# Sinkhorn-sorted attention feeding a top-1 expert layer: first sorting weights by 0/1 matmuls, later votes summed on GpSimd, TensorE order grouped by tile shape

## The chip, the cores and the metric

The kernel runs on one core of a Trainium2 chip. The metric is the device time of one execution in microseconds (us), given as the median of several runs. A core has five engines: TensorE (PE in the profile, with its weight loads as PEld), VectorE (DVE), ScalarE (ACT), GpSimd (POOL) and SyncE (SP). TensorE writes to PSUM, which has eight banks.

## The reference

```python
P = sort_net                                   # (4, 8, 8, 8): batch, head, block, block
for _ in range(5):                             # Sinkhorn
    P = P - np.max(P, axis=-1, keepdims=True)
    P = np.exp(P)
    P = P / (np.sum(P, axis=-1, keepdims=True) + 1e-09)
    P = P / (np.sum(P, axis=-2, keepdims=True) + 1e-09)
k_sorted = np.einsum('bhij,bhjcd->bhicd', P, k_b)   # 8 blocks of 96 rows, head_dim 64
v_sorted = np.einsum('bhij,bhjcd->bhicd', P, v_b)
scores = scale * np.matmul(q_b, k_sb.transpose(0, 1, 2, 4, 3))
...                                            # softmax in each block, times v_sb
x = attn_out.transpose(0, 2, 1, 3).reshape(3072, 512)
logits = x @ w_gate                            # 8 experts
expert_idx = np.argmax(logits, axis=1)
out[mask] = gate_w[mask, None] * (np.maximum(x[mask] @ w1[e], 0.0) @ w2[e])
```

Four batches, eight heads and 768 positions give 3,072 tokens of 512 features. Each expert has 1,024 hidden units.

## The kernel before

**The work.** Each of the four batches goes through attention and then through one expert. All inputs are read through GpSimd's DMA queue and turned to bf16 on the way. For a batch the kernel transposes q on TensorE (L593), sorts k (L614) and v (L641) by matmuls whose 0/1 structure holds the sorting weights, computes the scores of block i for all heads (`s`, L671), takes their exponential on ScalarE (L680), multiplies by the sorted v (`a`, L687), divides on VectorE (L697, L698), and transposes the result (`t`, L706) into `xT`. `route` (L731 to L755) computes the gate.

**The vote.** The kernel doesn't wait for the routing to load an expert. It sums v over all rows (`vote sum`, 24 matmuls, L538), projects the sum on the gate (`vote pick`, L547), reads the index of the maximum (L554, L555), and loads `w1` and `w2` of that expert (L338, L341), which it uses for the whole batch. Tokens that chose another expert are counted at the end; only if there are any does a loop over all experts run. For this input it doesn't run.

**The expert.** `h` is xT times w1 (four L764 matmuls for each of eight tiles and two halves), then a relu (L774 on ScalarE, L776 on VectorE), then `o`, hT times w2 (L769, in runs of four), weighed by the gate (L780, L782) and stored.

**First batch's sorting weights.** The Sinkhorn loop (L445 on ScalarE, L449 to L452 on VectorE) leaves `snb`, with batch and head on 32 partitions. `add_pk` and `add_pv` put it on 128 partitions: `rep` (L472, L498) copies the rows by a matmul with `expand_k` or `expand_v`, `sel` (L476, L502) multiplies by a mask `kj` or `vj`, `pt` (L479, L505) sums over j, and a last product with `ksel` or `vh` gives `pk` (L485) and `pv` (L509).

**v relay.** Before v can be sorted, VectorE copies it into another layout, `vr` (L578): four pieces for the first batch, two for the later ones.

**What sets the order.** Every step is a `Task` with a cost for each engine that can run it, the tasks it follows, a priority, and the PSUM banks it opens and closes. `Plan.schedule` plays a list schedule with these costs, and `emit` writes the instructions of each engine in that order; each engine then runs its own list strictly in order. The priorities put batch b at 100 b and the expert of batch b at 100 (b + 1), so that the expert of one batch and the attention of the next are interleaved. Tasks with a priority below -900 hold their place against others. `emit` puts matmuls on a tile of zeros (`idle`, L79) into gaps of TensorE's planned time. The loads of GpSimd's queue are one chain (L855 to L865): q0, v0, k0 in three parts, v1, then w1 and w2 of batch 0, q1, k1, then w1, w2, v, q, k of each following batch.

**Tile shapes on TensorE.** q, k and v groups write 64 columns of the array at a time (128*64 in the profile), the scores read 64 rows (64*128), and the rest uses 128 rows or columns.

Of the kernel before, what the change touches and what calls it, by code (L numbers as in the profile page):

```python
# [8 lines left out]
F32 = mybir.dt.float32  # L9
# [9 lines left out]
class Task:  # L19


    def __init__(self, name, cost, run, after, prio, opens, closes, lands):
        self.name, self.cost, self.run, self.prio = name, cost, run, prio
        self.after = [t for t in after if t is not None]
        self.opens, self.closes, self.lands = opens, closes, lands
        self.engine = self.start = self.end = self.behind = None
# [9 lines left out]
class Plan:  # L36
# [3 lines left out]
           ("dve", "pe"): 0.2, ("act", "dve"): 0.06, ("dve", "act"): 0.06,  # L40
           ("pe", "pe"): 0.0, ("act", "act"): 0.03, ("dve", "dve"): 0.04}
    LOOK = {"pe": 0.1, "act": 0.15, "dve": 0.15, "pool": 0.0, "sp": 0.0}
    FIRM = -900

    def __init__(self, dma_at=2.1):
        self.tasks, self.free = [], {}
        self.bank = [0.0] * 8
        self.dma_free = dma_at
        self.order = []

    def add(self, name, cost, run, after=(), prio=0, opens=None, closes=None, lands=None):
        t = Task(name, cost, run, after, prio, opens, closes, lands)
        self.tasks.append(t)
        return t
# [14 lines left out]
    def emit(self, nc, idle, psum, begin, warm, until):  # L69

        held, at = [0.0] * 8, begin
        for t in self.order:
            if t.engine == "pe":
                while t.start < until and t.start - at > 0.5:
# [3 lines left out]
                    us = 0.43 if at < warm else 0.217  # L78
                    nc.tensor.matmul(out=psum[:, free[-1], :], lhsT=idle[:, :128], rhs=idle,  # L79
# [27 lines left out]
    def schedule(self):  # L107
# [11 lines left out]
        while open_:  # L119
# [19 lines left out]
            for t in open_:  # L139
# [7 lines left out]
                for e, us in t.cost.items():  # L147
                    s = max(self.free.get(e, 0.0), bank_at)
# [9 lines left out]
                per.setdefault(e, []).append((s, t.prio, seq[t], t, end))  # L158
# [8 lines left out]
            t.engine, t.start, t.end = e, s, end  # L167
            self.free[e] = end
            if t.lands is not None:
# [4 lines left out]
                else:  # L174
                    t.end = end + 1.8
# [20 lines left out]
def kernel(  # L196
# [57 lines left out]
    v_in = [sb([P, HB, D], BF16, f"v_in{i}") for i in range(2)]  # L254
    qT = [sb([P, P, CS], BF16, f"qT{i}") for i in range(2)]
    ksT = [sb([P, X, 2, HP], BF16, f"ksT{i}") for i in range(2)]
    vr = [sb([P, D // 2, HP, 2], BF16, f"vr{i}") for i in range(2)]
# [20 lines left out]
    vh = sb([P, 2 * H], F32, "vh")  # L278
# [5 lines left out]
    expand_k = sb([BH, BH, NB * CQ], BF16, "expand_k")  # L284
    expand_v = sb([BH, BH, NB * 2], BF16, "expand_v")
# [84 lines left out]
    for i in range(2):  # L370
        e = "dve" if i == 0 else "pool"

        def zero_vr(e, i=i):
            engines[e].memset(vr[i][:, :, HB:, :], 0.0)

        def zero_ksT(e, i=i):
            engines[e].memset(ksT[i][:, :, :, HB:], 0.0)

        pads["vr", i] = add(f"zero vr{i}", {e: 0.5 if i == 0 else 1.0}, zero_vr, prio=-900 if i == 0 else 5)
        pads["ksT", i] = add(f"zero ksT{i}", {e: 0.5 if i == 0 else 1.0}, zero_ksT, prio=-899 if i == 0 else 5)  # L380
    mk_idle = add("idle", {"dve": 0.27}, lambda e: nc.vector.memset(idle, 0.0), prio=-950)  # L381
# [37 lines left out]
    def mask(name, ns, run, after, prio, e="dve"):  # L419
        return add(name, {e: ns}, run, after, prio=prio)  # L420

    m_vh = mask("vh", 0.27, lambda e: nc.vector.reduce_sum(
        vh.rearrange("p (f h) -> p f h", f=2),
        ident.rearrange("p (h j f) -> p f h j", h=H, j=NB), axis=AX.X), [mk_ident], -500)
    m_vm = mask("vmask", 0.17, lambda e: nc.vector.tensor_add(vmask, vh[:, :H], vh[:, H:]), [m_vh], -499)
    m_kc = mask("kc", 0.26, lambda e: nc.vector.reduce_sum(
        kc, ident.rearrange("p (x c) -> p x c", c=CQ), axis=AX.X), [mk_ident], -498)
    m_kj = mask("kj", 0.18, lambda e: nc.vector.reduce_sum(
        kj, kc.rearrange("p (h j) -> p j h", j=NB), axis=AX.X), [m_kc], -497)
    m_ks = mask("ksel", 0.26, lambda e: nc.vector.reduce_sum(  # L430
        ksel, ident.rearrange("p (h j c) -> p h c j", h=H2, j=NB), axis=AX.X), [mk_ident], -496)
    m_vj = mask("vj", 0.27, lambda e: nc.vector.reduce_sum(
        vj, ident.rearrange("p (h j f) -> p j h f", h=H, j=NB), axis=AX.XY), [mk_ident], -495)

    def run_expand(t, n, lo, hi):
        nc.gpsimd.tensor_copy(t[:, lo:hi], ident[:BH, lo:hi, None].to_broadcast([BH, hi - lo, n]))

    ek0 = add("expand k0", {"pool": 0.5}, lambda e: run_expand(expand_k, NB * CQ, 0, H), [mk_ident], prio=FIRST + 4)
    ev0 = add("expand v0", {"pool": 0.4}, lambda e: run_expand(expand_v, NB * 2, 0, H), [mk_ident], prio=FIRST + 4)
    ek1 = add("expand k", {"pool": 1.2}, lambda e: run_expand(expand_k, NB * CQ, H, BH), [mk_ident], prio=5)  # L440
    ev1 = add("expand v", {"pool": 0.8}, lambda e: run_expand(expand_v, NB * 2, H, BH), [mk_ident], prio=5)

    last = sn_at
    for it in range(5):
        last = add(f"exp {it}", {"act": 0.27}, lambda e: nc.scalar.activation(sn, sn, ACT.Exp), [last], prio=-990)  # L445

        def norm(view, dst, it, way):
            nonlocal last
            last = add(f"sum {way}{it}", {"dve": 0.22 if way == "r" else 0.26}, lambda e: nc.vector.reduce_sum(  # L449
                red[:, :, 0], view, axis=AX.X), [last], prio=-990)  # L450
            last = add(f"inv {way}{it}", {"dve": 0.19}, lambda e: nc.vector.reciprocal(red, red), [last], prio=-990)
            last = add(f"mul {way}{it}", {"dve": 0.25}, lambda e: nc.vector.tensor_mul(  # L452
# [9 lines left out]
    def add_pk(bs, prio, after, eng="dve"):  # L462
# [5 lines left out]
        def run_rep(e):  # L468
            t = bank(rep)[:, :n * NB * NB].rearrange("p (g i) -> p g i", g=n)
            for g in range(n):  # L470
                h0 = bs[0] * H + g * H2
# [17 lines left out]
    def add_pv(bs, prio, after, eng="dve"):  # L489
# [5 lines left out]
        def run_rep(e):  # L495
            t = bank(rep)[:, :n * NB * NB].rearrange("p (g i) -> p g i", g=n)
            for g, b in enumerate(bs):
                nc.tensor.matmul(out=t[:, g], lhsT=expand_v[:, b * H:(b + 1) * H].rearrange("p h x -> p (h x)"),  # L498
# [8 lines left out]
        for g, b in enumerate(bs):  # L507
            pv[b] = sb([P, 2 * H, NB], BF16, f"pv{b}")
            pv_at[b] = add(f"pv{b}", {eng: 0.27 if eng == "dve" else 0.5}, lambda e, b=b, g=g: engines[e].tensor_mul(  # L509
# [3 lines left out]
    add_pv([0], -980, [ev0], "pool")  # L513
    add_pk([0], -981, [ek0])

    def u32(ap):
        return ap.bitcast(U32)
# [9 lines left out]
    def add_attention(b):  # L529
# [5 lines left out]
        def run_vsum(e):  # L535
            t = bank(vb)[:, :H]
            for c in range(0, HB, 2):
                nc.tensor.matmul(out=t, lhsT=v_in[i2][:, c:c + 2, :].rearrange("p c d -> p (c d)"),  # L538
                                 rhs=vmask, start=(c == 0), stop=(c == HB - 2))

        vm = sb([P, H], BF16, f"vm{b}")
        t1 = add(f"vote sum{b}", {"pe": 0.65}, run_vsum, [v_at[b], m_vm], A - 20, opens=vb)
        t2 = add(f"vote vm{b}", {"act": 0.2, "dve": 0.2}, lambda e: copy(e, vm, bank(vb)[:, :H]), [t1], A - 20, closes=vb)

        def run_pick(e):
            for h in range(H):
                nc.tensor.matmul(out=bank(lb)[:, :E], lhsT=vm[:, h:h + 1].to_broadcast([P, P]),  # L547
                                 rhs=wv[:, h, :], start=(h == 0), stop=(h == H - 1))

        t3 = add(f"vote pick{b}", {"pe": 0.25}, run_pick, [t2, wv_a, wv_b], A - 20, opens=lb)  # L550
# [6 lines left out]
        t4 = add(f"vote read{b}", {"dve": 0.45}, run_read, [t3], A - 20, closes=lb)  # L557
# [6 lines left out]
        w1_at[b] = add(f"load w1.{b}", {"pool": 2.2}, run_w1, [t4, *relu_of.get(b - 2, [])], A - 20, lands=2.0)  # L564
# [7 lines left out]
        old = vsort_of.get(b - 2, [])  # L572
        cut = D // 4 if b else D // 8
        for d0 in range(0, D // 2, cut):
            def run_relay(e, d0=d0):
                dst = u32(vr[i2])[:, d0:d0 + cut, :HB, 0]
                src = u32(v_in[i2])[:, :, d0:d0 + cut]
                engines[e].tensor_copy(dst, src.rearrange("p c d -> p d c"))  # L578
            relays.append(add(f"relay{b}.{d0}", {"dve": 0.5 if b else 0.27}, run_relay,
                              [v_at[b], pads["vr", i2], *old], A - 10))  # L580
        v_done[b] = [t1, *relays]
# [369 lines left out]
```

## Time and profile before

| | us |
|---|---|
| median of 3 runs (167.73 to 168.97) | 168.0 |
| the profiled execution as a run | 170.06 |
| its span, first to last instruction | 168.4 |
| TensorE busy | 152.8 |
| ScalarE busy | 97.6 |
| VectorE busy | 84.4 |
| GpSimd busy | 28.6 |

In the profile, a line such as `L641` is a line of the kernel before. A group of instructions gives the busy time, the mean of one, and what ended the idle time before it. Matmuls are pipelined, so their durations overlap: what a group costs TensorE is read from the start of one group to the start of the next. The trace also holds the packets of each DMA queue, those of the instruction queues among them; adding up the bytes of the software queue gives the time at which each load ended.

### The profile page before, as it was taken

The page shows a single profiled execution, that of the slowest core. Times are in us where ns is not written, and L with a number is a line of the kernel's source. Part 1 is how long each engine was busy: PE and PEld are TensorE (multiplying, and loading weights), DVE is VectorE, ACT ScalarE, POOL GpSimd, SP SyncE. Part 2 cuts the span into 40 slices and gives each one's busy share as a digit, 9 for nine tenths or more (in the row PEclk, how much of TensorE's full clock was granted, in tenths as well). Part 3 has the DMA queues.
Part 4 walks back from the last instruction along what each step waited for, and adds up shares of the span by engine and source line. Part 5 has one row for each costly group of instructions (what it writes and reads, how often), then busy time and mean ns, then how long its engine had stood idle before and what let it go on. Part 6 is the DMA issues. An engine that isn't in the chain of part 4 may idle for free.

```text
span 168.4 us, 5239 instructions
## 1 busy us (share of the span) xinstructions
PE 152.8 (91%) x2246; PEld 95.1 (56%) x2261; DVE 84.4 (50%) x232; ACT 97.6 (58%) x147; POOL 28.6 (17%) x64
## 2 busy tenths in 40 slices
PE   6998559999999999999998999969999999999970
PEld 2366438768556656665555665745556655645540
DVE  5869685666524984443229664433227744420010
ACT  3174575557757745586757653747758736646440
POOL 6994700771000000800000001200000000000000
PEclk9999985599999999999999999999999999999999
DMA  3999999999999961699999603799131012005041
GB/s 30 209 202 221 159 209 197 203 210 208 207 219 239 257 133 66 127 221 203 221 207 250 154 5 123 111 230 208 25 125 62 4 62 101 30 0 187 0 152 47
DMA packets 13770, 24.51 MB, mean 146 GB/s; under 512 B 1328, under 2 KB 6448, under 8 KB 13744
## 3 DMA queue, kind: packets, MB, share of 16 engines
q0 software_dynamic: 9568, 17.83, 59.1%
q1 hardware_dynamic: 4032, 6.19, 10.5%
q8 instruction: 19, 0.31, 0.7%
q10 hardware_dynamic: 144, 0.13, 0.2%
q14 instruction: 7, 0.06, 0.1%
HBM read 35.68 MB, written 6.29 MB: 249 GB/s over the span
## 4 chain that ended last, share of the span: by engine, by line
PE 70%; DMA 17%; issue 5%; POOL 2%; DVE 2%; ACT 1%; DVEq 0%; ACTq 0%; POOLq 0%
PE psum L764 23%; PE psum L769 22%; DMA v_in<-in_v_dram 11%; DMA k_in<-in_k_dram 7%; PE psum L687 5%; PE psum L706 4%; PE psum L671 4%; PE psum L641 4%; PE psum L614 2%; PE psum L593 2%; ACT ex L680 1%; PE psum L538 1%; PE psum L731 1%; POOL k_in L313 1%; DVE vs L300 1%
## 5 line engine op out<-in xcount | busy, mean ns | idle before, releaser
L764 PE MATMUL psum<-xT,w 128*128 128x384 bf16 x256 | 50.9, 331 | 0.0
L769 PE MATMUL psum<-w,hT 128*128 128x512 bf16 (+1 forms) x186 | 43.9, 370 | 1.2 <-issue 0.6
L780 ACT ACTIVATE o<-psum,gws 128x512 f32<-128x512 f32 (+1 forms) x24 | 16.3, 679 | 28.0 <-PE psum L769 26.4
L764 PEld LDWEIGHTS <-w 128*128 128x128 bf16 x256 | 21.7, 99 | 12.6 <-issue 0.5
L769 PEld LDWEIGHTS <-hT 128*128 128x128 bf16 x200 | 17.9, 98 | 17.5
L680 ACT ACTIVATE ex<-psum 128x768 bf16<-128x768 f32 x32 | 25.4, 810 | 3.4 <-PE psum L671 2.6
L774 ACT ACTIVATE hT<-psum 128x384 bf16<-128x384 f32 x42 | 20.6, 490 | 10.1 <-PE psum L764 10.0
L698 DVE TENSOR_TENSOR xo<-psum,rec 96x512 bf16<-96x512 f32 x32 | 22.0, 687 | 1.3 <-DVE rec L697 0.3
L776 DVE TENSOR_SCALAR hT<-psum 128x384 bf16<-128x384 f32 x22 | 12.3, 557 | 12.1 <-PE psum L764 11.9
L298 ACT CAST vs<-psum 128x1024 bf16<-128x1024 f32 x13 | 13.1, 1019 | 6.9 <-PE psum L641 6.1
L300 DVE COPY xT<-psum 128x384 bf16<-128x384 bf16 x28 | 9.9, 353 | 12.2 <-PE psum L706 11.4
L338 POOL DMA_DIRECT2D w<-in_moe_w_dram x4 | 3.2, 804 | 73.6 <-DVE xT L300 61.9
L687 PE MATMUL psum<-vs,ex 128*128 128x65 bf16 x256 | 14.1, 201 | 0.9 <-ACT ex L680 0.9
L687 PEld LDWEIGHTS <-ex 128*128 128x128 bf16 x256 | 12.1, 103 | 4.6 <-ACT ex L680 1.3
L697 DVE RECIPROCAL rec<-psum 96x8 f32<-96x8 f32 x32 | 6.4, 200 | 14.8 <-PE psum L687 14.6
L641 PE MATMUL psum<-pv,vr 128*64 128x64 bf16 x512 | 10.9, 198 | 3.1 <-issue 3.1
L298 ACT COPY qT<-psum 128x1024 bf16<-128x1024 bf16 x11 | 11.0, 1013 | 4.0 <-PE psum L593 2.1
L641 PEld LDWEIGHTS <-vr 128*64 128x64 bf16 x512 | 9.4, 112 | 6.3 <-issue 5.8
L706 PE MATMUL psum<-ident,xo 96*128 96x96 bf16 x128 | 11.6, 217 | 0.8 <-DVE xo L698 0.8
L706 PEld LDWEIGHTS <-xo 96*128 96x128 bf16 x128 | 8.3, 102 | 5.4 <-DVE xo L698 1.8
L671 PE MATMUL psum<-qT,ksT 64*128 64x96 bf16 x256 | 10.7, 213 | 0.4 <-DVE vs L300 0.4
L79 PE MATMUL psum<-idle 128*128 128x512 bf16 x29 | 9.6, 498 | 1.5 <-DVE idle L381 1.3
(90 smaller groups left out, 132.4 us busy)
## 6 DMA issues: line engine op xcount, KB each, us to landing
w<-in_moe_w_dram POOLq DMA_DIRECT2D x8, 1024.0 KB, 14.4
out_dram<-o SPq DMA_DIRECT2D x23, 256.0 KB, 2.9
q_in<-in_q_dram POOLq DMA_DIRECT2D x4, 768.0 KB, 20.3
v_in<-in_v_dram POOLq DMA_DIRECT2D x4, 768.0 KB, 15.5
k_in<-in_k_dram POOLq DMA_DIRECT2D x3, 768.0 KB, 26.6
k_in<-in_k_dram POOLq DMA_DIRECT2D x3, 256.0 KB, 10.3
out_dram<-o ACTq DMA_DIRECT2D x1, 128.0 KB, 3.2
out_dram<-o SPq DMA_DIRECT2D x1, 128.0 KB, 2.6
```

Of the source, the lines that this page charges most:

```text
L298: nc.scalar.copy(dst, src)
L641: nc.tensor.matmul(out=t[f * HP:(f + 1) * HP, u, :], lhsT=vr[i2][:, d // 2, :, d % 2], rhs=pv[b][:, f * H:(f + 1) * H, :].rearrange("p h i ...
L671: nc.tensor.matmul(out=sc[:, r, h4 * BLK:(h4 + 1) * BLK], lhsT=ksT[i2][rows, x].rearrange("p f c -> p (f c)"), rhs=qT[i2][rows, x * CQ:(x ...
L680: te = add(f"exp{b}.{i}", {"act": 0.82}, lambda e, ex=ex, sbk=sbk: nc.scalar.activation(ex[:, :H * BLK].rearrange("p (t c) -> p t c", t=2) ...
L687: nc.tensor.matmul(out=av[:, h // 4, h % 4, :], lhsT=ex[:, h * BLK:h * BLK + P], rhs=vs[i2][:, h * NB + i, :D + 1], start=(h % 4 == 0), st ...
L698: nc.vector.tensor_mul(xo, av[:, :, :, :D], rec.to_broadcast([BLK, 2, 4, D]))
L706: nc.tensor.transpose(out=tp[:, dc, :], in_=xf[:, dc * P:(dc + 1) * P], identity=ident[:BLK, :BLK])
L764: nc.tensor.matmul(out=ps, lhsT=w1t[:, dc, fc * P:(fc + 1) * P], rhs=xT[:, dc, half * NH:(half + 1) * NH], start=(dc == 0), stop=(dc == DC ...
L769: nc.tensor.matmul(out=ps, lhsT=hT[:, fc, s * P:(s + 1) * P], rhs=w2t[:, fc, d0:d1], start=(fc == 0), stop=(fc == FC - 1))
L774: nc.scalar.activation(dst, src, ACT.Relu)
L776: nc.vector.tensor_scalar_max(dst, src, 0.0)
L780: nc.scalar.activation(dst, src, ACT.Copy, scale=gw)
```

## The change

1. **First batch's weights.** `add_pv([0])` and `add_pk([0])` go. Three scratch tiles (in hT buffers that are still free) are set to zero on ScalarE (`zero first`, three copies), filled with ones in a shifted pattern on GpSimd (`fill k`, `fill v`), and eight matmuls for each tile, one for each j and summed in PSUM, give what `pt` held. VectorE multiplies straight from PSUM into `pk` and `pv`. `expand_k` and `expand_v` lose the first batch's part.
2. **Votes.** Batch 0 keeps its 24 matmuls, now with a fixed priority. For batches 1 to 3 GpSimd adds the 48 rows of v in six additions (`vote add`), and one matmul with 64 columns sums over partitions.
3. **Modes.** Each TensorE task has a mode (`full`, `col`, `row`). The schedule adds 0.09 to a task that changes it, and gives 12 of priority to one that stays in `col` or `row`.
4. **Relays.** For the first batch two of the four pieces go to GpSimd; the later ones stay on VectorE.
5. **Loads.** v1 is no longer fifth: it follows w1 and w2 of batch 0.
6. **Fillers and costs.** `emit` fills gaps from 0.25 on (before 0.5), with 128 columns where the gap is at most 0.5, up to 32 of planned time (before 26). Many costs and some priorities are set anew, and the zeroing of the first ksT goes to GpSimd.

```diff
+                while t.start < until and t.start - at > 0.25:
+                    n = 512 if t.start - at > 0.5 else 128
...
+                    if e == "pe" and t.mode != self.mode:
+                        us += self.SWITCH
...
+                stay = e == "pe" and t.mode == self.mode != "full"
+                per.setdefault(e, []).append((s, t.prio - self.STAY * stay, seq[t], t, end))
...
-    add_pv([0], -980, [ev0], "pool")
-    add_pk([0], -981, [ek0])
...
+    def zero_first(e, t, w):
+        nc.scalar.copy(t.rearrange("p (a w) -> p a w", a=NB), idle[:BH, None, :w].to_broadcast([BH, NB, w]))
...
+        def run_pt(e, t, rep):
+            for j in range(NB):
+                nc.tensor.matmul(out=bank(rep)[:, :NB], lhsT=t[:, j * P:(j + 1) * P], rhs=snb[:, :, j],
+                                 start=(j == 0), stop=(j == NB - 1))
...
+            pk_at[0, g] = add(f"pk0.{g}", {"dve": 0.29}, lambda e, t=t, g=g: engines[e].tensor_mul(
+                t, ksel[:, :, None, :].to_broadcast([P, H2, NB, CQ]),
+                bank(banks[g])[:, None, :NB, None].to_broadcast([P, H2, NB, CQ])), [at[g], m_ks], -982 + g, closes=banks[g])
...
+            def run_add(e):
+                tt = nc.gpsimd.tensor_add
+                n = HB // 2
+                tt(v_tmp, v_in[i2][:, :n], v_in[i2][:, n:])
+                while n > 3:
+                    n //= 2
+                    tt(v_tmp[:, :n], v_tmp[:, :n], v_tmp[:, n:2 * n])
+                tt(v_tmp[:, 0], v_tmp[:, 0], v_tmp[:, 1])
+                tt(v_sum[i2], v_tmp[:, 0], v_tmp[:, 2])
...
+            def run_vsum(e):
+                nc.tensor.matmul(out=bank(vb)[:D, :H], lhsT=v_sum[i2], rhs=vmask, start=True, stop=True)
...
+            cost = {"dve": 0.82} if b else {"pool": 0.76} if d0 >= D // 4 else {"dve": 0.48}
...
-    seq.remove(v_at[1])
-    chain.append(v_at[1])
-    chain = chain[:5] + [v_at[1]] + seq
+    chain += seq
...
-    plan.emit(nc, idle, psum, 1.3, 5.5, 26.0)
+    plan.emit(nc, idle, psum, 1.4, 5.6, 32.0)
```

In the order that results, TensorE's list of the main part has q groups of 48 matmuls and v groups of up to 128 in a row where before they stood between L764 groups, and the scores come in groups of up to 24.

## The prediction

> **What bounds the kernel.** I read the page's header and slices first, then busy time by stage, then the timeline of TensorE, then the DMA packets added up by load.
>
> ```profile
> span 168.4 us, 5239 instructions
> ...
> PE 152.8 (91%) x2246; PEld 95.1 (56%) x2261; DVE 84.4 (50%) x232; ACT 97.6 (58%) x147; POOL 28.6 (17%) x64
> ...
> PE   6998559999999999999998999969999999999970
> ...
> PEclk9999985599999999999999999999999999999999
> ```
> TensorE is nearly full everywhere except around slices 4 to 6, and its clock is halved around slices 6 to 8.
>
> ```profile
> 20.30:24.26 3.96, 2.63 (x63) 1.87 (x60) 3.55 (x7) 3.90 (x6) 0.00 (x0) 1.00 1.11 209
> 24.26:34.50 10.24, 8.97 (x139) 7.25 (x140) 6.97 (x21) 4.27 (x7) 3.82 (x6) 0.50 1.16 200
> 34.50:41.00 6.50, 6.50 (x193) 5.06 (x191) 3.78 (x9) 4.58 (x8) 3.31 (x9) 1.00 1.09 209
> 41.00:163.20 122.20, 118.23 (x1571) 71.31 (x1581) 54.49 (x142) 76.10 (x114) 5.74 (x9) 1.00 0.62 135
> ```
> Columns: stretch, length, busy PE, PEld, DVE, ACT, POOL, clock, DMA share, GB/s. From 41 us to the last matmul at 163.2 TensorE alone sets the time: 118.2 of 122.2. The 10.24 us from 24.26 run at clock 0.50. The last output store after 163.2 costs 5.2.
>
> ```profile
> 99.84 0.76 PE L538 MATMUL psum<-vmask,v_in 128*128 128x8 bf16 x24
> 100.46 0.33 PE L706 MATMUL psum<-ident,xo 96*128 96x96 bf16 x4
> ...
> 105.32 0.81 PE L764 MATMUL psum<-xT,w 128*128 128x384 bf16 x4
> 106.06 0.70 PE L641 MATMUL psum<-pv,vr 128*64 128x64 bf16 x32
> 106.69 0.34 PE L706 MATMUL psum<-ident,xo 96*128 96x96 bf16 x4
> 106.87 0.81 PE L764 MATMUL psum<-xT,w 128*128 128x384 bf16 x4
> ...
> 111.00 0.61 PE L641 MATMUL psum<-pv,vr 128*64 128x64 bf16 x25
> 113.08 0.31 PE L641 MATMUL psum<-pv,vr 128*64 128x64 bf16 x7 [1.47 <-issue]
> ```
> From start to start: a vote sum takes 0.62; four L764 matmuls take 0.65 before a group of the same shape and 0.74 before the 64-column groups. Over all groups after 41 us, leaving a shape for another costs 0.09 to 0.10 and entering 0.01 to 0.02, so about 0.105 a change. The 1.47 is a hole inside one group of 32, with no wait in it.
>
> **What the skill says.** "TensorEngine Tiling (Array Packing)", Key Properties: changing the tiling mode drains TensorE. The trace agrees (0.105). "Runtime: NRT & Kernel Launch", Instruction fetch mechanics: instructions come in blocks of 256, by DMA, while the present block runs. The trace agrees and adds a price: the holes at 17.4, 24.2, 77.3 and 111.6 us all lie at instruction rows 448, 704, 2496, 3520 of TensorE's order, all 192 past a multiple of 256. The trace's records of the instruction queue show 16 KB fetches of 0.9 us, begun about 4 us after the previous boundary while data DMA runs (16.75, 23.06, 110.87) and at once where DMA is idle (after 120 us); TensorE goes on some 1.4 us after one lands. So a block under load can't follow its predecessor in less than about 6.4 us. "SBUF — State Buffer", Who interferes with whom: VectorE with two SBUF inputs and GpSimd reading SBUF exclude each other. The last L452 took 0.50 against a mean of 0.25 under a GpSimd copy, so the trace agrees.
>
> **The change, part by part.**
>
> *Mode grouping.* I classed each group in TensorE's order by its tile shape: 103 changes before, 73 after. 30 x 0.105 = 3.1 us. Nearly all lie in the full stage. Taken: -3.1.
>
> *Votes of batches 1 to 3.* 24 matmuls become one: 3 x (0.62 - 0.03) = -1.8. GpSimd gets 3,008 elements a vote in six adds. The trace has two-input GpSimd work only at 128 elements, 404 ns (L509). Bounds: 1.23 ns an element (slope of its copies, 300 ns at 128, 1086 at 768) gives 4.5 us; 3.16 (all 404 ns counted as elements) gives 9.5. "GPSIMD Engine Reference", 3.1 Elementwise, has about 2.6 cycles; at 1.2 GHz an estimate of 6.5 and six fixed parts of 0.14 (small memsets: 0.12) make 7.4. I take 7.4. It is in GpSimd's queue ahead of w1, w2 and the next v, q, k loads.
>
> *First batch's weights.* rep, sel and pt (0.2 + 0.29 + 0.29, then two of 0.25) become 24 matmuls (eight of L547 took 0.27 of issue: estimate 0.7) and products straight from PSUM. The chain gains some 0.5. But the first zero copy, about 1.05 us by a 1024-element ScalarE copy (1.01), sits between the table load's end (2.15) and the first exp, which started at 2.55: +0.65. Exp 4 no longer stands behind a qT copy: -0.9. Also the vote sum, formerly hidden at 11.95 us, now follows these matmuls: +0.6. And two relay pieces read SBUF on GpSimd from about 11.7, against the last sn products. Net: k sorting starts at about 14.1, as before. What follows waits for k's last third, landed 15.6 (L614 waited for it till 15.83), and for the fetch at row 448. That can't start later than the DMA's going idle at 15.6, so TensorE goes on at 15.6 + 0.9 + 1.4 = 17.9 (before 19.05). Four vs copies in a row on ScalarE (1.02 each) then put the first exp at about 21.3, as before (21.29). Taken: 0.
>
> *v1's load, no longer fifth.* It was issued at 8.00 and kept DMA full while the vote ran. Now w1 follows k, with nothing behind: the vote is read at about 15.5 (vm is behind three qT copies), plus 1.5 to issue as before (15.04 to 16.56), plus 1.9 to first bytes: DMA idle 15.6 to 18.9. By bytes of the queue w1 landed at 25.0, w2 30.4, q1 34.4, k1 38.2; now 24.2, 29.7, v1 33.8, q1 38, k1 42. TensorE used q1 at 40.4, k1 at 44.4; its new order puts them at about 44 to 47. Hidden. VectorE loses v1's relays (1.6) and a vote read from the first attention.
>
> *Half clock.* The fillers (10 of 128 columns, 0.5 us in all) are few beside the stage's dependency gaps, and 20.3:24.26 stays as thin as before. I leave the halved stage in. Removed there: the second vote sum and pick, at half speed 0.8 + 0.3; 0.4 above the count made already. Taken: -0.4.
>
> *Denser blocks.* With v and q grouped, the block of rows 2240 to 2496 holds 3.6 us of work, that of 3264 to 3520 4.3 us. Against 6.4 that is up to 2.8 + 2.1, where before 0.38 + 1.47 were lost: +3.0 at most, 0 if DMA is quiet. Half: +1.5.
>
> *Later w1 of batch 1.* Vote 1 is picked at about 47, w1 issued at 49 (before 30.4). With the old transfer times (k2's end 24.6 after w1's first bytes at 38.0) v2 lands at 66, q2 71, k2 76; TensorE wants k2 at about 76. It falls together with the fetch hole above. Taken: 0; 2 if both are late.
>
> Sum against the profiled span: 168.4 - 3.1 - 1.8 - 0.4 + 1.5 = 164.6. That execution took 170.06 as a run; the median of the runs shown is 168.0, 0.4 below its span. So 164.3 for the median (0.3 of rounding and tail left open).
>
> **The rivals.**
>
> *The clock holds* (0.25). For: VectorE in the halved stage waited 1.38 + 0.33 + 1.28 for TensorE, and 1.84 just after it, so the first attention could end up to 4.8 earlier at full speed, with w1 there at 24. Against: the fillers are few. 3.7 off: 160.6.
>
> *The saved work comes back as holes* (0.22). Both dense blocks stall in full (+1.5 above the sum) and k2 or VectorE, kept out by GpSimd's reads, costs 2 more: 167.8, within 1%. Against: at row 3520 DMA should be quieter, since k3 lands about 107.
>
> *GpSimd too slow, slower than before* (0.12). Place: the single matmul of the vote sum, which waits in TensorE's order with all behind it. Slack worked from the order: batch 1, adds begin about 38 (after nine products of 0.4) and TensorE arrives at 47.5: 9.5; batch 2, v2 at 66 to TensorE at 77: 11; batch 3 about 10. Each us beyond is lost three times. The gain of 3.8 is gone at (30.5 + 3.8)/3 = 11.4 us a vote; at 12.4 it gives 171. For: port exclusion both ways. Against: most VectorE inputs there are in PSUM.
>
> *The change doesn't do what it says* is not one: the orders show 73 changes and one matmul a vote.
>
> **How the numbers follow.** Likeliest: 164.3 (0.41), own range 162.5 to 166.3. About 1% is what a measurement here can tell from no change: 166.3 to 169.7. Faster: 0.41 x 0.92 + 0.25 + a little of the third case = 0.66. Same: 0.03 + 0.18 = 0.21. Slower: 0.13. The range reaches down to the clock case, 160.3, and up past the eaten gain, 168.8.
>
> **What would show it.** Right: single-matmul vote sums; L764 to L641 handovers fewer; TensorE's sum down by about 4; the halved stage still near 10 us; w1's first issue near 17 and the second near 49; holes of 1 to 3 us at rows 2496 and 3520. Wrong: no halved clock after 24 us (then about 160.6); a wait of TensorE for GpSimd's v_sum; adds above 11 us; a first exp of scores later than 22.3; a DMA wait before k2's matmuls longer than 2.

## The result and the profile after

The kernel after takes 173.87 us (median of 4 runs, 173.31 to 175.53) against 168.49 for the kernel before on the same chip: ratio 1.0324, 95% interval 1.022 to 1.0428. It was forecast at 164.3 and is slower. Ratios leave disturbed executions out, so they are not exactly the quotient of the medians beside them. The profiled execution took 173.76, with a span of 172.1.

The page of the kernel after, its header, slices and two of its groups:

```profile
span 172.1 us, 5205 instructions
...
PE   6879779993799999959999999489999999999970
...
PEclk9998799999579999996999999957999999999996
...
L594 POOL TENSOR_TENSOR v_tmp<-v_in 128x1536 bf16<-128x1536 bf16 x3 | 11.1, 3703 | 32.9 <-DMA v_in<-in_v_dram 32.9
...
L646 DVE COPY vr<-v_in 128x768 uint32<-128x768 uint32 (+1 forms) x8 | 14.5, 1849 | 3.8 <-DMA v_in<-in_v_dram 3.8
```

The same copies in the kernel before, the later batches' form alone:

```profile
L578 DVE COPY vr<-v_in 128x768 uint32<-128x768 uint32 x6 | 4.9, 826 | 3.2 <-DMA v_in<-in_v_dram 3.2
```

Counting slices from 0, the thin stage around slices 4 to 8 got better: no slice there is as thin as the 5 of before, and the stretch of 10.24 us at half clock is gone (one of 3.41 us now begins at 15.53, slices 3 and 4). In its place are three thin places (slices 9 and 10, 17, 25 and 26), one for each later batch, each with a lowered clock there or in the slice behind. And the relay copies (L646, one form of it the later batches') have become long: 1849 ns in the mean.

Busy time by stage, same stretches as before (length, PE, PEld, DVE, ACT, POOL, clock, DMA share, GB/s):

```profile
24.26:34.50 10.24, 9.99 (x155) 7.12 (x152) 8.05 (x21) 7.84 (x15) 3.31 (x9) 1.00 1.14 200
34.50:41.00 6.50, 5.54 (x133) 3.38 (x131) 5.38 (x5) 2.13 (x4) 4.85 (x2) 1.00 1.07 211
41.00:169.13 128.13, 117.64 (x1585) 73.93 (x1578) 64.39 (x136) 74.83 (x122) 28.38 (x32) 0.93 0.64 139
```

24.26 to 34.50 ran at full clock (0.50 before). From 41 us to the halved tail TensorE was busy 117.6 of 128.1, at a mean clock of 0.93, where before it was busy 118.2 of 122.2 at 1.00 (to its last matmul). So the time was gained in the first attention and lost, with interest, in three later places. The timeline shows two of these:

```profile
36.03 4.47 DVE L646 COPY vr<-v_in 128x768 uint32<-128x768 uint32 x2 [0.38 <-DMA v_in<-in_v_dram]
36.07 3.76 POOL L594 TENSOR_TENSOR v_tmp<-v_in 128x1536 bf16<-128x1536 bf16 x1 [2.09 <-DMA v_in<-in_v_dram]
37.42 1.21 PE L711 MATMUL psum<-pv,vr 128*64 128x64 bf16 x64
...
40.42 1.65 DVE L817 SCALAR_TENSOR_TENSOR key<-sh,rev 128x48 f32<-128x48 f32 x1
40.56 0.70 PE L711 MATMUL psum<-pv,vr 128*64 128x64 bf16 x32 [0.96 <-DVE vr L646]
...
44.20 1.06 PE L711 MATMUL psum<-pv,vr 128*64 128x64 bf16 x32 [2.94 <-DVE vs L310]
...
72.42 4.47 DVE L646 COPY vr<-v_in 128x768 uint32<-128x768 uint32 x2 [0.16 <-DMA v_in<-in_v_dram]
72.54 3.68 POOL L594 TENSOR_TENSOR v_tmp<-v_in 128x1536 bf16<-128x1536 bf16 x1 [14.85 <-DMA v_in<-in_v_dram]
...
76.95 1.92 PE L711 MATMUL psum<-pv,vr 128*64 128x64 bf16 x64 [2.13 <-DVE vr L646]
```

The landing of v releases two instructions at once: VectorE's relay and GpSimd's first addition. The first relay runs (0.84 us), the second lasts 3.7, until 0.7 after the end of the addition (in batch 3 it starts later and lasts 2.9). TensorE waits for its output, and later for a `vs` copy that stands behind it on VectorE. The next VectorE instruction with two SBUF inputs, L817, takes 1.65 (0.20 without additions beside it). By the clock records, stretches of 6.83, 3.41 and 6.83 us at half clock begin at 42.84, 76.97 and 111.10.

Two explanations fitted this best: the additions shut the relays out of a port (L, the lock), or the vote, now later, makes w1 and with it the next v land late, so that the holes are waits for a load (D, lateness). A third (M) was that the new order of TensorE's matmuls costs the time. v2 had landed at 52.5 before and landed at 71.4 after.

### The profile page after: what moved, and what is told of

The parts are those of the page before. It is cut to its first block, busy times and chain, and to the rows that moved or that the text cites. A ratio compares the mean times of both kernels' runs of the same rounds, so it can differ in the third digit from the quotient of the medians.

```text
span 172.1 us, 5205 instructions
## 1 busy us (share of the span) xinstructions
PE 152.1 (88%) x2222; PEld 97.4 (57%) x2222; DVE 92.9 (54%) x212; ACT 101.2 (59%) x164; POOL 54.7 (32%) x85
## 4 chain that ended last, share of the span: by engine, by line
PE 42%; DMA 30%; DVE 16%; issue 4%; ACT 2%; POOL 2%; POOLq 1%; DVEq 0%
DMA v_in<-in_v_dram 30%; PE psum L840 15%; PE psum L835 14%; DVE vr L646 8%; PE psum L661 3%; PE psum L711 3%; PE psum L683 2%; POOL w L351 1%; DVE red L456 1%; DVE sn L459 1%; PE psum L758 1%; DVE red L458 1%; PE psum L742 1%; POOLq L629 1%; DVE key L817 1%
## 5 line engine op out<-in xcount | busy, mean ns | idle before, releaser
L840 PE MATMUL psum<-w,hT 128*128 128x512 bf16 (+1 forms) x200 | 46.4, 376 | 0.0
L845 ACT ACTIVATE hT<-psum 128x384 bf16<-128x384 f32 x55 | 27.0, 491 | 17.5 <-PE psum L835 13.0
L851 ACT ACTIVATE o<-psum,gws 128x512 f32<-128x512 f32 (+1 forms) x21 | 14.2, 677 | 22.8 <-PE psum L840 18.0
L594 POOL TENSOR_TENSOR v_tmp<-v_in 128x1536 bf16<-128x1536 bf16 x3 | 11.1, 3703 | 32.9 <-DMA v_in<-in_v_dram 32.9
L711 PEld LDWEIGHTS <-vr 128*64 128x64 bf16 x512 | 11.7, 129 | 12.0 <-DVE vr L646 7.3
L646 DVE COPY vr<-v_in 128x768 uint32<-128x768 uint32 (+1 forms) x8 | 14.5, 1849 | 3.8 <-DMA v_in<-in_v_dram 3.8
L853 DVE TENSOR_SCALAR o<-psum,gws 128x512 f32<-128x512 f32 (+1 forms) x4 | 2.7, 683 | 24.8 <-PE psum L840 20.3
L310 DVE COPY xT<-psum 128x384 bf16<-128x384 bf16 x21 | 7.4, 353 | 10.1 <-PE psum L777 9.8
L597 POOL TENSOR_TENSOR v_tmp<-v_tmp 128x768 bf16<-128x768 bf16 (+2 forms) x9 | 10.7, 1185 | 0.7
L82 PE MATMUL psum<-idle 128*128 128x512 bf16 (+1 forms) x39 | 9.1, 383 | 1.9 <-DVE idle L389 1.3
```

Source lines behind the costliest of these rows:

```text
L594: tt(v_tmp, v_in[i2][:, :n], v_in[i2][:, n:])
L711: nc.tensor.matmul(out=t[f * HP:(f + 1) * HP, u, :], lhsT=vr[i2][:, d // 2, :, d % 2], rhs=pv[b][:, f * H:(f + 1) * H, :].rearrange("p h i ...
L840: nc.tensor.matmul(out=ps, lhsT=hT[:, fc, s * P:(s + 1) * P], rhs=w2t[:, fc, d0:d1], start=(fc == 0), stop=(fc == FC - 1))
L845: nc.scalar.activation(dst, src, ACT.Relu)
L851: nc.scalar.activation(dst, src, ACT.Copy, scale=gw)
```

## The experiments

The ratio is that to the kernel before on the same chip; a number of the first column stands for an experiment below.

| | votes 1 to 3 | order | v1's load | us | ratio, 95% interval |
|---|---|---|---|---|---|
| after | GpSimd | grouped | late | 173.87 | 1.0324 (1.022 to 1.0428) |
| 1 | TensorE | grouped | late | 164.2 | 0.9638 (0.9537 to 0.9738) |
| 1 again | TensorE | grouped | late | 164.75 | 0.9764 (0.9619 to 0.9909) |
| 2 | GpSimd, order of plan | grouped | late | 175.56 | 1.0361 (1.0274 to 1.0448) |
| 3 | TensorE, dead additions | grouped | late | 165.23 | 0.9734 (0.9667 to 0.9802) |
| 4 | GpSimd, relay on ScalarE | grouped | late | 165.07 | 0.9741 (0.9646 to 0.9837) |
| 5 | GpSimd after the relays | grouped | late | 167.23 | 0.9858 (0.9763 to 0.9953) |
| 6 | GpSimd | grouped | fifth | 171.16 | 1.0157 (1.0064 to 1.0251) |
| 7 | TensorE | ungrouped | late | 163.52 | 0.9715 (0.9642 to 0.9788) |
| 7 again | TensorE | ungrouped | late | 163.35 | 0.9744 (0.9648 to 0.9839) |
| 8 | before, votes on GpSimd | ungrouped | fifth | 173.24 | none |
| 9 | TensorE | grouped | fifth | 168.76 | 1.0051 (1.0015 to 1.0086) |
| 10 | TensorE | ungrouped | fifth | 168.92 | 1.0049 (1.0014 to 1.0083) |
| 11 | GpSimd | ungrouped | late | 168.18 | 0.9937 (0.9899 to 0.9976) |
| 12 | as 7, spare load fifth | ungrouped | late | 167.97 | 0.9921 (0.989 to 0.9952) |
| 13 | GpSimd, relay on ScalarE | ungrouped | late | 165.71 | 0.9815 (0.9719 to 0.9911) |
| 14 | GpSimd, short additions | grouped | late | 166.9 | 0.9806 (0.9707 to 0.9904) |

**1. Votes back on TensorE.**

```diff
-        if b == 0:
+        if True:
             def run_vsum(e):
                 for c in range(0, HB, 2):
...
-        n = D if b else P
+        n = P
```

> The kernel after, with the votes of batches 1 to 3 summed by 24 TensorE matmuls again, as in the kernel before; no adds on GpSimd, everything else stays. Theory L (GpSimd's first add of each vote keeps VectorE's relay copies off their common port, TensorE stands idle for the v products, and the idle time halves its clock): the relays go back to 0.8 us each, the halved stretches near 43, 77 and 111 us go, about 165 or less (173.9 less 3 x 3 us). Rival D (the vote comes late, so w1, w2 and the next v, q, k land late, and the holes are waits for these loads): the w1 loads are issued 6 us or more earlier and the same time is expected, 165 or less; this run does not tell L from D. Rival M (the new TensorE order, mode groups with denser instruction blocks, costs the time): no votes involved, 172 or more.

164.2: the loss is in the votes, and M, taken alone, is out as its cause. The relays take 0.82 again and no halved stretch lies at 77 or 111 us; near 43 one of 3.41 is left, behind a hole of 1.87 at 41.8 in which TensorE waits for nothing that the profile shows. L or D is not told.

**2. Additions after the relays, by the plan.**

```diff
+        if b:
+            v_read.after += relays
```

> The kernel after, with GpSimd's adds of a vote waiting until the two relay copies of the same batch are done; the adds themselves are unchanged, and the vote comes about 1.6 us later. L: the relays take 0.8 us each again, the waits of TensorE for them and the halved clock that follows go, 164 to 168. D: the vote is later still, so the loads are, no gain: 172 to 176. M: 172 to 175.

175.56, as D expected. But its trace has the relays at 1849 ns in the mean, as after: the edit moved the planned order only. Relay and addition share no output, so no wait was made, and GpSimd began at the landing of v. The run says nothing on the cause; number 5 does it with data.

**3. Early votes, additions kept as dead work.** The edit of 1, and GpSimd still adds, for nobody:

```diff
+            spare_add[b] = add(f"vote add{b}", {"pool": 7.6}, run_add, [v_at[b]], A - 20)
```

> The kernel after, with the votes summed by TensorE (loads issued early), but with the six adds of each vote still run on GpSimd at the landing of v, their result used by nobody (dead work). L: the relays stay shut out for 3 us a batch, TensorE waits for them as in the kernel after: 169 to 174. D: the loads come early, so most of the loss goes: 162 to 166. M: 172 or more.

165.23: L alone has failed. The relays are shut out here too:

```profile
66.06 3.69 POOL L611 TENSOR_TENSOR v_tmp<-v_in 128x1536 bf16<-128x1536 bf16 x1 [16.98 <-DMA v_in<-in_v_dram]
66.98 3.44 DVE L658 COPY vr<-v_in 128x768 uint32<-128x768 uint32 x1
67.75 1.09 PEld L723 LDWEIGHTS <-vr 128*64 128x64 bf16 x64
```

v2 landed at 64.2, not 71.4, so the first two v groups start at 67.75 with no wait, and the next two come only at 73.64. The lock is not free: TensorE waits 1.58 for the second relay near 39, 0.69 near 43, and 2.36 near 69 for an `xo` that stands behind the relay on VectorE. But no halved stretch follows, and the hole of 1.87 of number 1 is not there. The net is 1.0 us (165.23 - 164.2; 1.6 by the ratios). In the kernel after the holes at the v groups are 0.96 + 2.94, 2.13 and 0.99 + 1.83, and 17 us at half clock go with them.

**4. Relays of batches 1 to 3 on ScalarE.**

```diff
+                if e == "act":
+                    nc.scalar.copy(vr[i2][:, d0:d0 + cut, :HB, :],
+                                   v_in[i2][:, :, 2 * d0:2 * (d0 + cut)].rearrange("p c (d r) -> p d c r", r=2))
+                    return
...
-            cost = {"dve": 0.82} if b
+            cost = {"act": 1.5} if b
```

> The kernel after, with the relay copies of batches 1 to 3 done by ScalarE (as bf16, planned at 1.5 us each) and no longer by VectorE; the adds stay on GpSimd at the landing of v. L: ScalarE is not shut out, so the copies take what they take when undisturbed (1 to 2 us) and the waits shrink; ScalarE loses 2 to 4 us a batch to them: 165 to 170. D: the loads are as late as before, 172 to 176. M: 172 to 175.

165.07: D alone has failed as well. The votes still come from GpSimd's additions, v2 lands at 66.1, later than in 1 (59.6) or 3. The copies take 1.55 us each, and the first addition 3.13 instead of 3.70. But without the lock TensorE is further on when it votes, and v2 is 5 us earlier than after: lateness is less here too. So less lateness without the lock costs 1 to 2 us net (0.9 by the medians, 1.7 by the ratios), the lock with little lateness about the same, and both together 9. That suggests an interaction, I: a late v2 or v3 lands when TensorE wants it, the time for which the relay is shut out becomes TensorE's, and the clock halves after it. For batch 1 it can't be the lateness: v1 is as early in 1 as after (34.4 and 34.9). Its two waits of 0.96 and 2.94 in the kernel after come from the relay and from what stands behind it on VectorE, and no run takes batch 1 apart from batches 2 and 3.

**5. A wait made of data.** GpSimd reads two elements of each relay's output into scratch before it adds (the edit of 2 is in as well).

```diff
+                for d0 in range(0, D // 2, D // 4):
+                    nc.gpsimd.tensor_copy(v_tmp[:1, 0, :2], vr[i2][:1, d0, 0, :])
```

> The kernel after, with a wait made of data: before the first add of a vote, GpSimd copies two elements of each of the two relay outputs of the batch into the sum's scratch tile (overwritten at once), so the adds can't begin before both relays are done. (The earlier run meant to do this changed only the planned order and let GpSimd start as before.) Theory I (interaction: the late vote makes v land only when TensorE wants it, and then the shut-out relays are exposed; either alone costs about 1 us): relays 0.82 us each again at the landing of v, votes 1.7 us later than in the kernel after; 164 to 168. Rival D (lateness alone): 172 to 177. Rival L (lock alone): 163 to 166.

167.23, in I's range, although the additions of batch 1 end later than after (45.2 against 44.4) and v2 lands no earlier (72.0).

```profile
36.04 1.57 DVE L648 COPY vr<-v_in 128x768 uint32<-128x768 uint32 x2 [0.59 <-DMA v_in<-in_v_dram]
...
37.22 1.20 PE L713 MATMUL psum<-pv,vr 128*64 128x64 bf16 x64
...
38.00 3.09 POOL L596 TENSOR_TENSOR v_tmp<-v_in 128x1536 bf16<-128x1536 bf16 x1
...
38.42 2.69 DVE L830 SCALAR_TENSOR_TENSOR gws<-picks,top,gates 128x6 f32<-128x6 f32 x1
...
42.30 1.05 PE L713 MATMUL psum<-pv,vr 128*64 128x64 bf16 x32 [2.28 <-DVE vs L310]
...
74.38 2.22 PE L713 MATMUL psum<-pv,vr 128*64 128x64 bf16 x128 [1.77 <-DVE vr L648]
```

Two relays take 1.57 together, not 4.47. Two things remain. One is a wait of 1.77 for the late v itself (batch 2). The other is the lock again, on another instruction: in batch 1 a VectorE instruction of six elements with its inputs in SBUF (L830; the same one took 0.25 us in the kernel after) lasts 2.69, to the end of the addition; the `vs` copy stands behind it, TensorE waits 2.28 for that copy, and 3.41 us at half clock begin at 42.36. So 5 is not lateness alone.

**6. v1's load fifth again, all else as after.**

```diff
-    chain += seq
+    seq.remove(v_at[1])
+    chain += [v_at[1]] + seq
```

> The kernel after, with the load of v of batch 1 put back as fifth, ahead of the first w1 and w2, as in the kernel before; the GpSimd adds stay. I: v1 lands near 20, its adds run during the first sort and attention, the vote of batch 1 is out by about 30, so the second w1 and with it v2 land some 15 us earlier; batches 1 and 2 get their slack back, batch 3 perhaps not: 164 to 169. L alone (the load's place doesn't matter): 172 to 175. If the first attention needs w1 early, its load behind v1 costs up to 3 us and the clock halves again near 24 us.

171.16, outside both theories' ranges. v2 lands at 61.9, ten earlier, and the later holes shrink, as I says; but the clock is halved for 17.07 us from 15.2. In the first attention the lock shows as well: VectorE's first relay of v1 begins at 22.48 and lasts 5.32, past two GpSimd copies and the addition that follows them, and TensorE waits 0.95 for an `xo` behind it. What the load's place itself does there, 9 and 10 measure without GpSimd's votes.

**7. Votes on TensorE, grouping off.**

```diff
-    FIRM, SWITCH, STAY = -900, 0.09, 12
+    FIRM, SWITCH, STAY = -900, 0.0, 0
```

> The first experiment (votes of batches 1 to 3 on TensorE), with the grouping by tile shape switched off in the planner (its price of a change and its preference for staying set to 0): 97 changes of shape in TensorE's order and not 67. By the price of the prediction, 0.105 us a change: 30 x 0.105 = 3.1 us more than the first experiment, 167.3. Rival (grouping worth nothing, the gain lies elsewhere): 164. Rival (an ungrouped order is also thinner around the first attention, and the clock halves there): 169 or more.

163.52: grouping shows no gain. 30 more shape changes cost no time in the sum.

**8. Before, with the votes on GpSimd alone.** The additions and the single matmul of the change are put into the kernel before; nothing else is moved.

> The kernel before, with one part of the change alone: the votes of batches 1 to 3 summed by GpSimd's adds. The load of v1 stays fifth, TensorE's order stays ungrouped. I: loads are early enough at first (v1 lands at 19.5), so the lock costs about 1 us a batch and the late vote little until batch 3; against it 1.8 us of TensorE saved: 168 to 172 (before 169.5). L alone: 175 or more, as every batch loses 3 us at its relays. Prediction's step: 167.7 (1.8 saved, adds hidden).

Runs from 169.43 to 176.48, median 173.24; too scattered for a verdict. All four are above 168.49, the median of the kernel before, so the part alone does not look like a gain; its size stays open.

**1 and 7 again, 9 and 10: grouping against the place of v1's load, on one chip.** 9 and 10 put the load fifth as in 6.

> The first experiment again (votes on TensorE, grouped order, v1's load after the first w1 and w2), beside the three that follow: a square of two sides, grouped or not, and v1's load late or fifth. 164.2 as before. By the price of a shape change it should be 3.1 us faster than its ungrouped partner; by theory H (the grouped order packs the q, k and v products so densely that TensorE runs out of fetched instructions, and the clock halves after the hole) within 1.5 us of it.

> The same without grouping (97 changes of shape, not 67), a second time. By the price of a change: 167.3. By theory H: 163.5 as before, with no halved stretch between 10 us and the end.

> The first experiment (votes on TensorE, grouped) with v1's load put back as fifth, ahead of the first w1. Theory F (with nothing queued behind k the DMA engines are idle from 15.6 to 18.9, so TensorE's next instruction blocks arrive at once; with v1 there they arrive late, TensorE has holes near 17.5 and 24 us, and the clock halves): 168 to 170, halved for 7 us or more between 15 and 35. The prediction's step (the place of the load is hidden, 0): 164.

> Votes on TensorE, no grouping, v1's load fifth: of the change there stay only the first batch's weights by 0/1 matmuls, the relay in four pieces, shorter fillers and altered planned costs. F: 167 to 169, halved for 7 us or more between 15 and 35, so that next to nothing is left of the gain over the kernel before (168.5). Rival (the new first-batch weights brought the gain): 164.

164.75, 163.35, 168.76, 168.92. Down the columns: the load's move is worth 4.0 (168.76 - 164.75) and 5.6 (168.92 - 163.35). Across: grouping is worth 0.2 and -1.4, within what the runs can tell. And number 10, which keeps the first batch's new weights, its two relay pieces on GpSimd (four pieces there are in the kernel before too) and the fillers, is within 1% of before: together these are worth about nothing.

The timeline of TensorE, number 10 first, then the second run of 7; up to these matmuls the two have the same ones in the same order:

```profile
18.35 0.35 PE L711 MATMUL psum<-pv,vr 128*64 128x64 bf16 x11 [2.02 <-issue]
...
21.95 0.33 PE L758 MATMUL psum<-vs,ex 128*128 128x65 bf16 x5
25.37 1.21 PE L758 MATMUL psum<-vs,ex 128*128 128x65 bf16 x19 [3.09 <-issue]
```

```profile
17.53 0.35 PE L711 MATMUL psum<-pv,vr 128*64 128x64 bf16 x11 [0.96 <-issue]
...
21.13 0.96 PE L758 MATMUL psum<-vs,ex 128*128 128x65 bf16 x16
```

The holes are at rows 448 and 704 of TensorE's order, 192 past a multiple of 256. In 10 the records of the instruction queue show the two fetches beginning at 16.02 and 22.85; in 7, with the DMA engines idle after k, at 15.10 and 18.58, and the second hole is gone. 10 then runs at half clock for 10.24 us from 23.87, as before (24.26); 7 has no halved stretch from 10 us to 160. So hole and long half clock come and go together with the load's place; that the hole begins the half clock is not shown, since in before it begins with the hole (24.24) and not after it.

What grouping can cost shows in 1 (second run) and in 9, whose q groups of batch 2 stand in one piece:

```profile
70.99 0.39 PE L661 MATMUL psum<-ident,q_in 128*64 128x128 bf16 x8
73.55 2.35 PE L661 MATMUL psum<-ident,q_in 128*64 128x128 bf16 x40 [2.16 <-issue]
```

```profile
75.07 0.67 PE L661 MATMUL psum<-ident,q_in 128*64 128x128 bf16 x17
78.79 1.34 PE L661 MATMUL psum<-ident,q_in 128*64 128x128 bf16 x31 [3.06 <-issue]
```

Both are at row 2496, and 3.41 us at half clock follow each. 7 and 10 have no such hole there. 2.2 to 3.1 of idle time, and up to half of 3.41, are as much as the 30 saved changes (3.1 us) would have given. It is not the whole account: in the first profile of 1, the same kernel, the hole at this row is 0.57 and no half clock follows, and yet that execution (164.18) was not faster than 7's (163.11); there 3.41 us at half clock stand at 23.27 and 43.76. The price of a change has no run that tests it alone.

**11. After, grouping off.** The edit of 7 on the kernel after.

> The kernel after with the grouping switched off alone (79 changes of shape, not 71); the votes stay on GpSimd. Theory I (late v and a shut-out relay) does not need the grouped order: TensorE still wants v's products when v lands, 170 to 175. If the dense v groups were needed for the loss (four v groups in a row drain what the relays feed), 164 to 167.

168.18: between the two expectations. The votes on GpSimd cost 4.8 here (168.18 - 163.35) and 9.1 in the grouped order (173.87 - 164.75). Both differences are between chips; by the ratios they are 3.3 and 9.4. Lock and lateness don't need the grouped order, but it makes what they cost two to three times as much. In the profile of 11 (171.38, 3.2 over the kernel's median) the holes at the v groups are 0.97, 0.73 + 2.41 and 0.99, 5.1 in all against 8.9 in the kernel after, and one halved stretch of 3.41 goes with them; 6.83 us at half clock from 23.72, in the first attention, also lengthened that execution. The difference is largest in batch 1, where the kernel after has its four v groups nearly in a row.

**12. A spare load.** Number 7 with v1 loaded a second time, fifth, read by nobody. Engines do the same work in the same order up to the relays of batch 1.

```diff
-    chain += seq
+    spare_load = add("spare load", {"pool": 0.73}, lambda e: nc.gpsimd.dma_start(
+        out=v_in[1], in_=v[1].rearrange("h (x c) d -> (h x) c d", c=HB)), prio=1, lands=1.5)
+    v_at[1].after.append(spare_load)
+    chain += [spare_load] + seq
```

> The second ungrouped kernel (votes on TensorE, v1 after w2), with a load of v1 added as fifth, ahead of the first w1, that nobody reads (the same tile is loaded again in its place). TensorE's first 1120 instructions, and what the other engines do up to the relays of batch 1, stay as they are; only the DMA queue is full between 15.6 and 19. F: the fetches start late, holes of 1.5 to 3 us near 17.5 and 24, halved clock for 7 to 10 us: first attention 4 to 5 us longer, 168 to 171 (some of it perhaps by the later q1, k1). Rival (v1's early relays and its vote read on VectorE, in the middle of the first attention, made the loss): 163.5 to 165.5.

167.97, just under F's range and far above the rival's. The fetches start at 16.01 and 22.82, as in 10, there are holes of 1.20 and 1.78 at the two rows, and halved stretches of 6.83 us at 15.16 and 25.40. At its 380th matmul TensorE is 4.1 us behind the second run of 7, at its 500th 6.0, and no further behind at the end (5.2), so the loss lies in the first attention. A full DMA queue is enough; VectorE's relief is not needed. (The first halved stretch begins ahead of the first hole, at 17.16, and kernels with the late load have 3.41 us there too, as 1 again from 15.05: its beginning is not the hole's doing.)

**13. Number 4 without grouping.**

> Votes on GpSimd, relays of batches 1 to 3 on ScalarE, no grouping: a candidate to stand beside the best so far (163.4). If the 1.8 us of TensorE that the GpSimd votes save count, 162 to 163; if late loads and ScalarE's 1.5 us copies eat them, 164 to 166.

165.71: the 1.8 us of TensorE that GpSimd's votes save buy nothing here, even with the relays out of the way (ScalarE's longer copies may have taken part of it). TensorE has three holes of 1.36, 2.01 and 2.17 us at rows 1472, 2496 and 3520.

**14. Short additions.** The kernel after, its first addition cut in eight; every engine's planned order unchanged.

```diff
-                tt(v_tmp, v_in[i2][:, :n], v_in[i2][:, n:])
+                for c in range(0, n, n // 8):
+                    tt(v_tmp[:, c:c + n // 8], v_in[i2][:, c:c + n // 8], v_in[i2][:, n + c:n + c + n // 8])
```

> The kernel after, with the first addition of each later vote (1536 elements, 3.7 us) cut into eight of 192 elements; the planned order of every engine stays as it was. If one instruction of GpSimd holds the common port from its start to its end (so the second relay waits for the end of the first addition, which is what the trace of the kernel after shows in all three batches), the second relay waits for one short addition only: relays of 0.8 to 1.6 us, TensorE's holes near 40, 75 and 110 us shrink, 165 to 169, at the price of about 1 us more for each vote. If GpSimd's additions win the port each time however short they are, the second relay still ends with the last of the eight pieces, 3.7 us or more: 173 to 176.

166.9, 7 us less than after, though GpSimd works longer:

```profile
37.84 1.94 DVE L647 COPY vr<-v_in 128x768 uint32<-128x768 uint32 x2 [0.27 <-DMA v_in<-in_v_dram]
37.89 5.35 POOL L595 TENSOR_TENSOR v_tmp<-v_in 128x192 bf16<-128x192 bf16 x8 [1.99 <-DMA v_in<-in_v_dram]
39.34 1.20 PE L712 MATMUL psum<-pv,vr 128*64 128x64 bf16 x64
```

Two relays in 1.94, in the midst of eight additions that take 5.35 (3.76 in one piece). The second relay of a batch now lasts at most 1.2: it waits for one short instruction and not for the whole addition. That it gets in after the first one is not a rule: in 6 a relay waited through three GpSimd instructions in a row. The price shows too, as TensorE waits 0.98 at 46.4 for `v_sum`. (This profiled execution took 169.3, 2.4 over the kernel's median; its first attention had halved clock.)

The fastest kernel tried is number 7: 163.52 and 163.35, ratios 0.9715 and 0.9744. It keeps the moved load, the first batch's weights and relay pieces and the fillers, and drops the votes on GpSimd and the grouping.

## Why the prediction was wrong, step by step

**Votes of batches 1 to 3** is the step that failed most. The additions were sized well: 7.4 us estimated, 8.3 measured (7.2 where the relays were on ScalarE), below the 11.4 at which the forecast's slow rival was to decide, and TensorE did not wait for the vote sum. Yet the votes, priced at -1.8, cost 9.1. The prediction knew the port rule and set it aside in that rival ("most VectorE inputs there are in PSUM"). It overlooked the one large VectorE copy from SBUF to SBUF, the relay, which the same event releases as the addition. The Trainium skill, "SBUF — State Buffer", Who interferes with whom, says that of a VectorE copy in its two-port mode and GpSimd whoever issues first has the pair "for the whole instruction; the other **fully blocks**". The traces agree: the second relay lasts 3.7 us beside one long addition, 0.82 without, 1.2 beside short ones. (Whether the relay runs in that mode no view shows.) Small instructions with their inputs in SBUF are shut out as well (L817 after, L830 in 5), and the `vs` copies stand behind them.

**Later w1 of batch 1** was costed at 0. Issue came at 53.76 (forecast 49), v2 landed at 71.4 (66), q2 76.3 (71), k2 81.5 (76). The prediction compared only k2 with TensorE's need. v2 is wanted first, at 73.6, and relays stand between. With the relays free the lateness costs 1 to 3 us (experiments 4 and 5, the second with a lock left in it); it took away slack that would have hidden part of the lock.

**v1's load** was costed at 0 and is worth 4.0 to 5.6. Its numbers were near: the DMA engines idle from 15.6, first w1 issue 17.37 (forecast near 17), v1 landed at 34.9 (33.8), hidden. The prediction even used the idle time for the fetch at row 448 (TensorE on again at 17.81; forecast 17.9). It did not carry this one block further: the fetch for row 704, which made the hole at 24.24 before, then starts at 19.00 and not at 23.06, before w1's bytes fill the queue.

**Half clock**: "left in", and the 10.24 us are gone (3.41 at 15.53 came). That was the rival *the clock holds*, which did not name what holds it. The fillers are in 10 as well, which halves, so it is not they; the hole at row 704 goes together with the half clock. In before it can't have begun it, as both begin at 24.2: the thin stage ahead, busy 2.63 of 3.96, must have had a part. The Trainium skill, "TensorE: Matmul & The Clock Gate", Part 1: The HAM clock gate, has the clock set over windows of about 3.4 us; the halved stretches here are 3.41, 6.83, 10.24, 17.07 and 20.48, which agrees. The rule in its section on HAM oscillation, "no PE-idle gaps >~3.4µs", is too generous here: a hole of 2.16 in a dense stretch was followed by 3.41 at half clock.

**Mode grouping** (-3.1) and **denser blocks** (+1.5) gave together about 0. Denser blocks were right in their mechanism: the hole at row 2496 came with 0.6 to 3.1 us in 1 and 9 (forecast up to 2.8). The half clock that followed it in two of their three profiles was not in the sum. The price of a change stays untested. In the kernel after itself there is none at that row: TensorE waited for the relay, and the block was there. The Trainium skill, "Runtime: NRT & Kernel Launch", Instruction fetch mechanics, calls crossing a block "mostly hidden"; here holes of up to 3.09 us stand at such rows while data DMA runs.

**First batch's weights**: forecast 0, measured 0 together with relay pieces and fillers (experiment 10). k sorting began at 13.97 (forecast 14.1).

**The sum as measured**, in the order 10, 9, 1, after: 168.9, then -0.2 for grouping, -4.0 for the load, +9.1 for GpSimd's votes. The terms are not independent: the votes cost 2.4 in the grouped order with the load fifth (171.16 - 168.76, two chips), where v2 lands ten earlier than after.

What stays open: the cost of the votes alone on the kernel before (experiment 8 scattered), and how the 9.1 split between idle time and the clock that it halves; no run changed the one and kept the other.

## What to carry to other kernels

When work moves to GpSimd, list every VectorE instruction that reads and writes SBUF and can fall beside it, small ones too: those that the same event releases, and those behind them; cut the GpSimd work into short instructions or order it behind, and check with a real data dependency, not with a planner's order. A delay and a lock that are each hidden by the same slack must be costed together. In an unrolled kernel, mark the rows at which TensorE's instruction blocks end: a load that is queued there can cost more than its own time, and denser code between two such rows gained nothing here.

## What the runs showed that was not expected

- A data load that nobody reads, on an otherwise unchanged kernel, costs 4.6 us (167.97 against 163.35, two chips; 3.0 by the ratios). Two instruction fetches start 0.9 and 4.2 us later, and half clock goes with it.
- Holes of 1 to 3 us can be followed by 3.4 to 6.8 us at half clock. After the hole of 2.16 in 1 that is up to 1.7 more (half of 3.41), so a stall can cost nearly twice what it shows. Not each one does: after the 2.36 of experiment 3 the clock stayed.
- Where the hole lies decides. The clock records of a trace change on a grid of 3.41 us. Of the stretches of that grid at full clock between 26 and 150 us, in all 18 profiles, 13 had TensorE busy at most 0.46 of the time, and half clock followed every one; of six at 0.49 to 0.51 it followed two; of the 605 above, none. The 2.36 of experiment 3 fall across two stretches, busy 0.62 and 0.69. Ahead of 26 us this doesn't hold: there half clock followed stretches busy up to 0.88, and the cause stays open.
- GpSimd's addition of two bf16 operands takes 3.1 us for 1,536 elements a partition undisturbed and 0.30 for 64: an estimate of 1.9 ns an element and 0.18 us fixed ((3.13 - 0.30) / 1,472 and 0.30 - 64 x 0.0019). ScalarE's bf16 relay of 1,536 elements takes 1.55 us where VectorE's as 768 words takes 0.82.
